# Keys, values and x rows in longer runs, routing buffers and list weights moved, in an attention and mixture-of-experts kernel

## The chip, the cores and the metric

The program runs on one core of a Trainium2 chip. The metric is the device time of one execution in microseconds (us), the median of the runs shown. The core has TensorE (PE, with PEld for its weight loads), VectorE (DVE), ScalarE (ACT), GpSimd (POOL) and SyncE (SP). Each engine works through its own queue in order. Plain transfers are issued by SyncE here, indirect ones by GpSimd; all of them share 16 transfer engines.

## The reference

Attention with 32 memory slots for each of 8 batches and 8 heads (576 positions, 64 values a head), and then a layer of 8 experts in which each of the 4608 rows goes to its two best. Softmaxes and the noise of the gate are cut short here.

```python
a   = softmax(phi, over the positions)               # 8 x 8 x 576 x 32
k_m = einsum('bhsm,bhsd->bhmd', a, k)                # 32 x 64 a head
v_m = einsum('bhsm,bhsd->bhmd', a, v)
x   = softmax(q @ k_m.T / 8) @ v_m                   # rows of 8 * 64 = 512
noisy = x @ w_gate + log1p(exp(x @ w_noise)) * noise # 4608 x 8
top2  = the two largest of noisy, weights by softmax
for e in range(8):
    h = maximum(x[rows of e] @ w1[e], 0)             # 512 -> 1024
    out[rows of e] += weight * (h @ w2[e])           # 1024 -> 512
```

## The kernel before

**Attention.** The work runs over 16 units `u` (a batch and half of its heads). `a_load` brings keys and values of a unit into `kvs` (1 MB and a rest of 128 KB), `p_load` phi, `q_load` q. `a_exp`, `a_tr1`, `a_tr5`, `a_kv` make the slots' keys `kk` and values `vm`; `a_kt` and `a_g` transpose them and multiply the values by the gate's matrix (`a_g`: one product of 128x64, a mask `gt`, a sum over heads); `a_s` makes the scores. Two batches form a pair P (four pairs). Over 20 groups `n` of rows (five a pair) `c_sc`, `c_soft1`, `c_soft2`, `c_tr` do the softmax, and `c_av` makes a block `j` of 128 rows of x (`xr`), with the gate's 16 logits beside it, writes the rows to `xs` in DRAM and adds the logits of both halves into `lg`. A pair has 9 blocks, so there are 36 x writes.

**Routing.** `gate(P, j0, j1)` finds the two best experts of each row of a pair and the row's place in the expert's list (`gidx`), and puts row number and weight into `gent`. Then GpSimd scatters them into the list `lst` in DRAM, two indirect transfers a block: 18 for a pair, and for the last pair 10 and 8 in two calls. `gidx` and `gent` lie in the pool `gs`, which has one buffer.

**Experts.** `lists` reads an expert's list back (`lt`), `gather` fetches its rows from `xs` (`gtile`, GT tiles), halves them into two f16 parts (`ghalf`) and transposes them by a transfer into `xt`. `mm1` is the first layer (L678), `mm2` the second (L705), `put` adds the result to `out` by an indirect transfer (L728). `wt` scales the list's weights (`wlu`). `w_load` and `w_prep` bring an expert's weights (`stg`) and split them into two f16 parts `wh`, `wl` (L569, L570), after a maximum (`wam`, L555) and its scale (`wsa` to `wsc`). The groups 0, 1 and 2 of expert 0 (two tiles each, which need the lists of the first pairs only) are computed while the attention and the routing still run; group 3 (the rest of expert 0) needs the whole list, and all further groups follow it.

**What sets the order.** `unit`, `group`, `weights`, `routing` and `early` give every step a due time from the table `PRI`; the steps are written in that order and a scheduler places the instructions in each engine's queue by priority. `BUF` sets the numbers of buffers and, in `zg`, `zr`, `r0`, `r1`, `m0` to `m2`, after which attention group zero writes, weight splits and early groups may start (`after`). `zero_out` writes zeros to the whole output, 256 KiB each; the first TRASH rows of `xs` and `out` take entries that no row fills.

## Time and profile before

| | us |
|---|---|
| median of 3 runs (lowest, highest) | 1042.14 (1041.88, 1044.54) |
| the profiled execution | 1048.34 |
| its span, first to last instruction | 1046.5 |
| TensorE busy | 962.7 (92%) |
| VectorE busy | 535.2 (51%) |
| ScalarE busy | 370.5 (35%) |
| GpSimd busy | 298.4 (29%) |

Shares of a whole span hide the stages: the attention fills about the first 195 us, the early groups of expert 0 run between 196 and 285 us, and the rest is the experts. Where the profile names a wait, it names the time an engine stood idle in front of an instruction and what ended that. Source lines are those of the kernel before; in the new one they are up to 12 higher.

### The profile page before, as it was taken

The page shows a single profiled execution, that of the slowest core. Times are in us where ns is not written, and L with a number is a line of the kernel's source. Part 1 is how long each engine was busy: PE and PEld are TensorE (multiplying, and loading weights), DVE is VectorE, ACT ScalarE, POOL GpSimd, SP SyncE. Part 2 cuts the span into 40 slices and gives each one's busy share as a digit, 9 for nine tenths or more (in the row PEclk, how much of TensorE's full clock was granted, in tenths as well). Part 3 has the DMA queues.
Part 4 walks back from the last instruction along what each step waited for, and adds up shares of the span by engine and source line. Part 5 has one row for each costly group of instructions (what it writes and reads, how often), then busy time and mean ns, then how long its engine had stood idle before and what let it go on. Part 6 is the DMA issues. An engine that isn't in the chain of part 4 may idle for free.

```text
span 1046.5 us, 15053 instructions
## 1 busy us (share of the span) xinstructions
PE 962.7 (92%) x5632; PEld 500.4 (48%) x5632; DVE 535.2 (51%) x1395; ACT 370.5 (35%) x760; POOL 298.4 (29%) x262
## 2 busy tenths in 40 slices
PE   4898975895799998999999999999999999999995
PEld 3555643563344445444644464445444544454452
DVE  2578888535476254984272349544523682232211
ACT  3466655313242232532242244324222542221211
POOL 1000633776246304222323132223132213211121
PEclk9699977798899999999999999999999999999998
DMA  9999999555988439756546257845453626430221
GB/s 291 331 327 327 267 330 302 113 118 84 238 148 196 95 37 176 204 129 100 107 131 110 42 91 206 170 88 82 131 101 78 124 57 110 66 51 11 31 32 25
DMA packets 143642, 147.93 MB, mean 141 GB/s; under 512 B 92944, under 2 KB 102224, under 8 KB 143568
## 3 DMA queue, kind: packets, MB, share of 16 engines
q1 hardware_dynamic: 124112, 107.02, 39.9%
q0 software_dynamic: 19456, 39.93, 22.0%
q8 instruction: 45, 0.74, 0.3%
q14 instruction: 29, 0.24, 0.1%
HBM read 86.77 MB, written 40.22 MB: 121 GB/s over the span
## 4 chain that ended last, share of the span: by engine, by line
PE 56%; DMA 8%; issue 6%; DVE 6%; POOL 2%; ACT 1%; SPq 0%; POOLq 0%; ACTq 0%; DVEq 0%
PE mp L678 27%; PE ps L705 27%; DMA xt<-ghalf 3%; DVE wl L570 2%; DMA lst<-gent,gidx 2%; DVE wam L555 2%; PE ps L715 2%; DMA stg<-in_w 2%; DMA out<-y,lt 1%; POOL out L728 1%; POOL lst L514 1%; DVE ghalf L654 1%; DVE hl L686 0%; ACT ghalf L651 0%; DVE hh L685 0%
## 5 line engine op out<-in xcount | busy, mean ns | idle before, releaser
L678 PE MATMUL mp<-xt,wh 128*128 128x512 f16 (+2 forms) x1408 | 280.2, 336 | 11.3 <-issue 6.6
L678 PEld LDWEIGHTS <-wh 128*128 128x128 f16 x1600 | 152.5, 99 | 143.6 <-issue 26.6
L728 POOL DMA_INDIRECT out<-y,lt x80 | 128.7, 1609 | 259.8 <-ACT y L709 231.9
L705 PE MATMUL ps<-wh,hl 128*128 128x512 f16 x528 | 200.0, 379 | 1.6 <-DVE hl L686 1.6
L705 PE MATMUL ps<-wl,hh 128*128 128x512 f16 x528 | 199.8, 379 | 0.0
L685 DVE CAST hh<-r 128x512 f16<-128x512 f32 (+3 forms) x200 | 72.1, 364 | 248.8 <-ACT r L684 247.7
L705 PE MATMUL ps<-wh,hh 128*128 128x512 f16 x528 | 195.5, 379 | 1.3 <-DVE hh L685 1.3
L640 POOL DMA_INDIRECT gtile<-xs,lt x80 | 91.0, 1138 | 332.5 <-DVE ghalf L654 292.0
L684 ACT ACTIVATE r<-mp 128x512 f32<-128x512 f32 (+3 forms) x200 | 97.0, 492 | 246.9 <-PE mp L678 175.4
L705 PEld LDWEIGHTS <-hh 128*128 128x128 f16 x1152 | 112.3, 98 | 135.1 <-DVE hh L685 4.6
L678 PE MATMUL mp<-xt,wl 128*128 128x512 f16 (+2 forms) x704 | 151.4, 337 | 0.0
L654 DVE TENSOR_TENSOR ghalf<-gtile,ghalf 128x512 f16<-128x512 f32 x80 | 55.1, 691 | 126.1 <-ACT ghalf L651 125.9
L686 DVE TENSOR_TENSOR hl<-r,hh 128x512 f16<-128x512 f32 (+3 forms) x200 | 111.3, 562 | 4.6
L651 ACT ACTIVATE ghalf<-gtile 128x512 f16<-128x512 f32 x80 | 50.0, 628 | 170.7 <-DMA xt<-ghalf 155.6
L514 POOL DMA_INDIRECT lst<-gent,gidx x72 | 73.0, 1014 | 129.3 <-DVE pe L385 102.8
L678 PEld LDWEIGHTS <-wl 128*128 128x128 f16 x800 | 76.9, 99 | 58.6 <-issue 1.3
L705 PEld LDWEIGHTS <-hl 128*128 128x128 f16 x576 | 56.3, 98 | 74.7 <-issue 5.7
L555 DVE TENSOR_REDUCE wam<-stg 128x1 f32<-128x512 f32 x128 | 81.1, 678 | 20.4 <-DMA stg<-in_w 20.2
L709 ACT ACTIVATE y<-ps,wlu 128x512 f32<-128x512 f32 x66 | 44.7, 681 | 125.0 <-PE ps L705 92.0
L570 DVE SCALAR_TENSOR_TENSOR wl<-stg,wsc,wh 128x512 f16<-128x512 f32 x112 | 76.4, 743 | 1.9 <-ACT wh L569 1.7
L569 ACT ACTIVATE wh<-stg,wsc 128x512 f16<-128x512 f32 x112 | 70.1, 708 | 14.2 <-DVE wsc L336 13.8
L417 PE MATMUL xp<-vb,at 128*128 128x272 f32 (+1 forms) x160 | 50.6, 477 | 14.7 <-ACT xr L419 14.0
(160 smaller groups left out, 723.2 us busy)
## 6 DMA issues: line engine op xcount, KB each, us to landing
stg<-in_w SPq DMA_DIRECT2D x64, 512.0 KB
kvs<-in_kv SPq DMA_DIRECT2D x16, 1024.0 KB
out<-zt SPq DMA_DIRECT2D x38, 256.0 KB
qs<-in_q_t SPq DMA_DIRECT2D x16, 576.0 KB
xs<-xr SPq DMA_DIRECT2D x36, 256.0 KB
phs<-in_phi_t SPq DMA_DIRECT2D x16, 288.0 KB
kvs<-in_kv SPq DMA_DIRECT2D x16, 128.0 KB
gtile<-xs,lt POOLq DMA_INDIRECT x80
```

What stands on the lines that cost most here:

```text
L514: sc = G.indirect_dma_start(out=lst[:, :], out_offset=bass.IndirectOffsetOnAxis(ap=idx[:, j, k:k + 1], axis=0), in_=ent[:, j, k, :], in_of ...
L555: d = V.tensor_reduce(am[:, c:c + 1], ss[c], axis=AX.X, op=OP.max, apply_absolute_value=True)
L569: A.activation(wh[:, cs], ss[c], AF.Identity, scale=sc)
L570: V.scalar_tensor_tensor(wl[:, cs], ss[c], sc, wh[:, cs], op0=OP.mult, op1=OP.subtract)
L640: G.indirect_dma_start(out=gts[i][:n], out_offset=None, in_=xs[0:seen, :], in_offset=bass.IndirectOffsetOnAxis(ap=LT[e][:n, t, 0:1].bitcas ...
L654: V.tensor_tensor(gh[:n, 1], gts[i][:n], gh[:n, 0], OP.subtract)
L678: d = mark["mm1", g if e == 0 else None] = T.matmul(ps[:, :n], ww[:, c * FF + f * 128:c * FF + (f + 1) * 128], xt[:, xo + c, :n], start=(k ...
L684: A.activation(r[:, :n], ps[:, :n], AF.Relu, scale=HC)
L685: V.tensor_copy(hh[:, f, :n], r[:, :n])
L686: V.tensor_tensor(hl[:, f, :n], r[:, :n], hh[:, f, :n], OP.subtract)
L705: T.matmul(ps, hs[:, i * 128:(i + 1) * 128], ws, start=(k == 0), stop=(k == 8 * m - 1))
L728: d = G.indirect_dma_start(out=out[:, :], out_offset=bass.IndirectOffsetOnAxis(ap=LT[e][:n, t, 0:1].bitcast(I32), axis=0), in_=y[:n], in_o ...
```

## The change

Keys and values are laid out on the host so that one partition's four rows of a unit are one run of 8 KB (they were four runs of 2 KB); x rows are written as one run of 2 KB (they were two of 1 KB), for which the logits of one half stand ahead of the values and those of the other behind them; TRASH is 128 instead of 256. `a_g` makes four products of 32 rows by 16 columns and one copy, in place of the product, mask and sum. The first five normalisations of the softmax (GN) run on GpSimd; GL and GV are 0 and move nothing. `gidx` and `gent` have three buffers, `gtile` four. `wt` for expert 0's last tiles is written behind the first layer of group 3. `PRI` and some pacing numbers of `BUF` (`zg`, `zr`, `m1`, `r0`, `r1`) have other values.

```diff
-TRASH = 256
+TRASH = 128
-BUF = dict(kvs=3, phs=3, qs=2, et=2, es=3, pe=4, at=3, xr=4, st0=1, st1=1, ptr=3, px=2, mps=3, xa=3, w1=8, w2=8, zg=9,
-           ws=1, m0=16, m1=18, m2=19, r0=6, r1=6, zr=5)
+BUF = dict(kvs=3, phs=3, qs=2, et=2, es=3, pe=4, at=3, xr=4, st0=1, st1=1, ptr=3, px=2, mps=3, xa=3, w1=8, w2=8, zg=8,
+           ws=1, m0=16, m1=19, m2=19, r0=14, r1=3, zr=6)
...
-GT = 3
+GT = 4
+GN, GL, GV = 5, 0, 0
...
-        nc.sync.dma_start(kvs[:, 0:4], kv[b, 0:512, g].rearrange("(c p) h x -> p c h x", p=128))
-        nc.sync.dma_start(kvs[:64, 4], kv[b, 512:576, g])
+        nc.sync.dma_start(kvs[:, 0:4].rearrange("p c h x -> p (c h x)"),
+                          kv[b, g, 0:512].rearrange("(p c) x -> p (c x)", c=4))
+        nc.sync.dma_start(kvs[:64, 4].rearrange("p h x -> p (h x)"), kv[b, g, 512:576])
...
-        T.matmul(p4[:, 0, 0:64], VT[u], wg_sb[:, g, :], start=True, stop=True)
-        gt = sm.tile([128, 4, 16], F32, name="gt")
-        V.tensor_tensor(gt, p4[:, 0, 0:64].rearrange("p (h c) -> p h c", h=4), vmask[:, :, 0:16], OP.mult)
         vb = wk.tile([128, 272], F32, name="vb", bufs=8)
-        V.tensor_reduce(vb[:, 256:], gt.rearrange("p h c -> p c h"), axis=AX.X, op=OP.add)
+        for h in range(4):
+            T.matmul(p4[h * 32:(h + 1) * 32, 0, 0:16], VT[u][:, h * 32:(h + 1) * 32],
+                     wg_sb[:, g, h * 16:(h + 1) * 16], start=True, stop=True)
+        A.activation(vb[:, 0:16] if g == 0 else vb[:, 256:], p4[:, 0, 0:16], AF.Copy)
...
-        V.tensor_tensor(pe[:, 0:k], pe[:, 0:k], ss[:, 0:k, None].to_broadcast([128, k, M]), OP.mult)
+        (G if n < GN else V).tensor_tensor(pe[:, 0:k], pe[:, 0:k], ss[:, 0:k, None].to_broadcast([128, k, M]), OP.mult)
...
-        nc.sync.dma_start(xs[r0:r0 + 128, :].rearrange("p (g d) -> p g d", g=2), xr[:, :, 0:256])
+        nc.sync.dma_start(xs[r0:r0 + 128, :], xr[:, 16:528])
...
-        idx = gs.tile([128, NJ, 2], I32, name="gidx")
-        ent = gs.tile([128, NJ, 2, 2], F32, name="gent")
+        idx = gs.tile([128, NJ, 2], I32, name="gidx", bufs=3)
+        ent = gs.tile([128, NJ, 2, 2], F32, name="gent", bufs=3)
...
-        if e == 0 and t1 <= 6:
+        if e == 0:
             after(d, "mm1", t0 // 2)
...
     lists(0, 6, NTL + 1)
-    wt(0, 6, NTL + 1)
...
         for f in range(8):
             mm1(e, g, f)
             step_side(2)
+        if (e, g) == (0, 3):
+            wt(0, 6, NTL + 1)
```

The table of due times moves instructions in every queue. Three places show what the prediction speaks of.

SyncE's queue at the first list read of expert 0 (`lt<-lst 128x2x2`), before: `xs<-xr` are x writes, `out<-zt` zero writes, the transposes those of group 0.

```order
L150 DMA out<-zt 128x512 x5
L423 DMA xs<-xr 256x1x256 x2
L150 DMA out<-zt 128x512
L423 DMA xs<-xr 256x1x256
L150 DMA out<-zt 128x512 x2
L593 DMA lt<-lst 128x2x2 x2
L423 DMA xs<-xr 256x1x256 x2
L655 DMA_TRANSPOSE stg<-ghalf 128x8x128 x2
```

The same place after:

```order
L153 DMA out<-zt 128x512 x5
L431 DMA xs<-xr 128x512
L153 DMA out<-zt 128x512
L431 DMA xs<-xr 128x512
L601 DMA lt<-lst 128x2x2 x2
L431 DMA xs<-xr 128x512 x4
L663 DMA_TRANSPOSE stg<-ghalf 128x8x128 x2
```

Counted from the queue's start, the list read stands behind 31 x writes and 38 zero writes before, and behind 27 and 37 after; ahead of group 0's transposes stand two x writes more than before.

GpSimd's queue from the gathers of group 0 to the last scatters, before: `gent` is the counter that starts a routing's entries, `lst<-gent,gidx` the scatters, `out<-y,lt` the adds to the output.

```order
L640 DMA gtile<-xs,lt 128x512 x3
L514 DMA lst<-gent,gidx 37888x2 x13
L640 DMA gtile<-xs,lt 128x512
L514 DMA lst<-gent,gidx 37888x2 x5
L495 IOTA gent 128x10
L514 DMA lst<-gent,gidx 37888x2 x10
L728 DMA out<-y,lt 4864x512
L640 DMA gtile<-xs,lt 128x512 x2
L728 DMA out<-y,lt 4864x512
L495 IOTA gent 128x8
L514 DMA lst<-gent,gidx 37888x2 x8
```

And after:

```order
L522 DMA lst<-gent,gidx 37888x2 x18
L503 IOTA gent 128x8
L648 DMA gtile<-xs,lt 128x512 x4
L522 DMA lst<-gent,gidx 37888x2 x28
L648 DMA gtile<-xs,lt 128x512 x2
L736 DMA out<-y,lt 4736x512 x2
L522 DMA lst<-gent,gidx 37888x2 x8
L648 DMA gtile<-xs,lt 128x512 x3
L648 DMA gtile<-xs,lt 64x512
```

The counters have moved ahead of the gathers, and the scatters of the third pair and of the first part of the last pair stand in one row.

VectorE's queue around the scaling of expert 0's last list weights (`wlu<-lt,wu 128x3` and `64x1`), before:

```order
L555 TENSOR_REDUCE wam<-stg 128x1 x4
L654 TENSOR_TENSOR ghalf<-gtile,ghalf 128x512
L561 TENSOR_REDUCE wam_3802<-wam 128x1
L617 TENSOR_SCALAR wlu<-lt,wu 128x3
L331 TENSOR_REDUCE wsa<-pb 128x1
L332 TENSOR_SCALAR wsa<-wsa 128x1
L621 TENSOR_SCALAR wlu<-lt,wu 64x1
L334 TENSOR_SCALAR wsb<-wsa 128x1
L336 TENSOR_SCALAR wsc<-wsb 128x1
L570 SCALAR_TENSOR_TENSOR wl_3814<-stg,wsc,wh_3813 128x512 x3
```

And after (the part of 128x3 stands further back, behind six of group 3's eight casts):

```order
L339 TENSOR_SCALAR wsc<-wsb 128x1
L693 CAST hh<-r 128x256
L694 TENSOR_TENSOR hl<-r,hh 128x256
L578 SCALAR_TENSOR_TENSOR wl_3829<-stg,wsc,wh_3828 128x512 x2
L625 TENSOR_SCALAR wlu<-lt,wu 128x2
L578 SCALAR_TENSOR_TENSOR wl_3829<-stg,wsc,wh_3828 128x512 x6
L693 CAST hh<-r 128x256 x2
L694 TENSOR_TENSOR hl<-r,hh 128x256 x2
L629 TENSOR_SCALAR wlu<-lt,wu 64x1
L662 TENSOR_TENSOR ghalf<-gtile,ghalf 128x512
```

The scale and the split of expert 1's first weights now stand ahead of the first scaling that needs the last list.

## Rows read from the trace of the kernel before

**Rows 1.** Windows: engines' busy us (and instructions), granted clock, transfer share, GB/s.

```profile
core 0: us, PE busy (x) PEld busy (x) DVE busy (x) ACT busy (x) POOL busy (x), PEclk, DMA share, GB/s
125.00:165.00 40.00, 32.00 (x236) 19.30 (x234) 35.18 (x135) 22.74 (x59) 21.06 (x23) 0.83 1.09 308
165.00:180.00 15.00, 7.05 (x21) 3.54 (x21) 14.04 (x49) 9.02 (x21) 3.52 (x4) 0.75 1.05 332
275.00:300.00 25.00, 18.35 (x87) 8.71 (x86) 14.77 (x28) 5.71 (x10) 7.42 (x7) 0.86 1.08 238
325.00:350.00 25.00, 25.00 (x128) 11.28 (x127) 13.47 (x25) 7.37 (x13) 9.84 (x7) 1.00 0.53 91
500.00:600.00 100.00, 100.00 (x532) 49.14 (x531) 41.36 (x82) 29.47 (x52) 26.18 (x21) 1.00 0.48 96
```

**Rows 2.** Timeline of SyncE: start, duration, transfer issued.

```profile
179.30 1.09 SPq L593 DMA_DIRECT2D lt<-lst  x2
180.50 9.12 SPq L423 DMA_DIRECT2D xs<-xr  x2
```

**Rows 3.** Timeline of GpSimd, with the idle time ahead and what ended it.

```profile
184.83 1.00 POOL L640 DMA_INDIRECT gtile<-xs,lt  x1 [9.79 <-DMA lt<-lst]
...
188.66 1.00 POOL L514 DMA_INDIRECT lst<-gent,gidx  x1 [0.30 <-issue]
189.97 0.98 POOL L514 DMA_INDIRECT lst<-gent,gidx  x1 [0.30 <-issue]
...
211.98 0.96 POOL L514 DMA_INDIRECT lst<-gent,gidx  x1 [0.31 <-issue]
214.73 0.14 POOL L495 IOTA gent<- 128x10 int32 x1 [1.79 <-DMA lst<-gent,gidx]
215.69 0.98 POOL L514 DMA_INDIRECT lst<-gent,gidx  x1 [0.82 <-DVE gai L501]
...
235.15 1.00 POOL L514 DMA_INDIRECT lst<-gent,gidx  x1 [0.28 <-POOL gent L495]
...
244.87 0.97 POOL L514 DMA_INDIRECT lst<-gent,gidx  x1 [0.31 <-issue]
...
253.28 1.01 POOL L640 DMA_INDIRECT gtile<-xs,lt  x1 [5.51 <-DMA lt<-lst]
```

**Rows 4.** Timeline of VectorE: indices of two routings, and the list's scaling.

```profile
182.46 0.18 DVE L502 CAST gidx<-gai 128x18 int32<-128x18 f32 x1
...
232.68 0.17 DVE L502 CAST gidx<-gai 128x8 int32<-128x8 f32 x1 [6.83 <-DMA lst<-gent,gidx]
...
252.36 0.23 DVE L617 TENSOR_SCALAR wlu<-lt,wu 128x3 f32<-128x3 f32 x1 [9.85 <-DMA lt<-lst]
```

**Rows 5.** Timeline of TensorE and ScalarE: first matmul, a result, waits.

```profile
196.05 1.04 PE L678 MATMUL mp<-stg,wh 128*128 128x256 f16 x4 [1.30 <-DMA stg<-ghalf]
...
219.39 0.69 ACT L709 ACTIVATE y<-mp,wlu 128x512 f32<-128x512 f32 x1 [3.58 <-PE mp L705]
...
253.39 1.95 ACT L569 ACTIVATE wh<-stg,wsc 128x512 f16<-128x512 f32 x3 [9.94 <-DVE wsc L336]
...
255.65 1.01 PE L678 MATMUL mp<-stg,wh 128*128 128x256 f16 x4 [5.61 <-ACT r L684]
...
285.60 1.65 PE L678 MATMUL mp<-xt,wh 128*128 128x448 f16 x4 [6.65 <-issue]
```

**Rows 6.** Groups by line and form: busy us, mean ns, idle before.

```profile
L275 PE MATMUL tr<-kvs,es 128*32 128x128 f32 x512 | 22.4, 322 | 8.9 <-DMA kvs<-in_kv 6.7 <-DVE gt L320 1.4 <-DVE kb L296 0.9
L396 DVE TENSOR_TENSOR pe<-pe,ss 128x512 f32<-128x512 f32 x16 | 11.0, 686 | 0.1
L294 ACT ACTIVATE vt<-tr 64x128 f32<-64x128 f32 x16 | 4.2, 265 | 0.3 <-PE tr L292 0.2
L322 DVE TENSOR_REDUCE vb<-gt 128x16 f32<-128x64 f32 x16 | 4.0, 252 | 0.0
L320 DVE TENSOR_TENSOR gt<-tr,vmask 128x64 f32<-128x64 f32 x16 | 3.5, 221 | 4.1 <-PE tr L318 4.0
```

**Rows 7.** Transfer queue in 10:55, 140:145, 165:180 us: packets, MB, share.

```profile
q1 hardware_dynamic: 6921, 14.83, 104.2%
...
q1 hardware_dynamic: 968, 2.05, 104.5%
...
q1 hardware_dynamic: 3440, 4.93, 103.1%
```

More of the change, by code (lines that the diff above doesn't have):

```diff
@@ L27 @@
 TAIL = CAP - NTL * 128
[L28 removed]
+TRASH = 128
 ZC = 512
 ZERO_AT = 20
[L31 to L38 removed]
+PRI = dict(D=5.82512, p=-1.14871, kv=-1.26659, q=-2.4532, exp=-1.09005, tr1=-2.82213, tr5=-2.85978, kvm=0.83783,
+           kt=1.0766, s=2.13563, g=2.0709, v=3.89957, v1=2.83229, sc=-2.28787, s1=-0.02984, s2=0.281, tr=-0.49952,
+           av=1.31436, avb=1.42743, gate=0.6, g2=0.5622, gs=0.99413, x0=0.22977, md=0.72156, md1=0.2297, fill=5.7433,
+           prep=2.87573, prd=0.4427, wl=1.01221, wl3=3.40386, pr1=6.05278, z=4.13465, zd=0.20212, d0=-1.38568,
+           d1=-0.31647, d2=0.35338, d3=-0.20179, sc0=1.77362, sc1=-0.24397, sc2=-0.03774, sc3=0.13919, f0=0.11614,
+           f1=0.2, g0=1.24719, g1=0.39992, prep0=3.62472, prd0=0.55109)
+BUF = dict(kvs=3, phs=3, qs=2, et=2, es=3, pe=4, at=3, xr=4, st0=1, st1=1, ptr=3, px=2, mps=3, xa=3, w1=8, w2=8, zg=8,
+           ws=1, m0=16, m1=19, m2=19, r0=14, r1=3, zr=6)
 NEED = (1, 1, 2)
[L41 removed]
+GT = 4
 HC = 2.0 ** -14
 WEXP = 2.0 ** 9
+GN, GL, GV = 5, 0, 0
 SBITS = float((2 * 127 + 9) << 23)
@@ L355, in a_v @@
         for g in range(2):
-            vb = VB[2 * b + g][:, 0:256].rearrange("p (h d) -> p h d", h=4)
+            vb = VB[2 * b + g][:, 16 - 16 * g:272 - 16 * g].rearrange("p (h d) -> p h d", h=4)
             vm = VM[2 * b + g]
-            V.scalar_tensor_tensor(vb, vm[:, None, :].to_broadcast([128, 4, D]), s, vmask, op0=OP.mult, op1=OP.mult)
+            if b < GV:
+                G.tensor_scalar(vm, vm, s, None, op0=OP.mult)
+                G.tensor_tensor(vb, vm[:, None, :].to_broadcast([128, 4, D]), vmask, OP.mult)
+            else:
+                V.scalar_tensor_tensor(vb, vm[:, None, :].to_broadcast([128, 4, D]), s, vmask, op0=OP.mult, op1=OP.mult)
     JS = ((0, 1), (2, 3), (4,), (5, 6), (7, 8))
@@ L412, in c_av @@
             LG[P] = wk.tile([128, NJ, 16], F32, name="lg")
-        xr = wk.tile([128, 2, 272], F32, name="xr", bufs=BUF["xr"])
+        xr = wk.tile([128, 544], F32, name="xr", bufs=BUF["xr"])
         for g in range(2):
@@ L916, in layout @@
     a["phi_t"] = c(phi.reshape(B, 2, 4, S, M).transpose(0, 2, 4, 1, 3).reshape(B, 128, 2, S))
-    a["kv"] = c(np.concatenate([k[..., None, :], v[..., None, :]], axis=-2)
-                .reshape(B, 2, 4, S, 2 * D).transpose(0, 3, 1, 2, 4))
+    x = (np.concatenate([k[..., None, :], v[..., None, :]], axis=-2)
+         .reshape(B, 2, 4, S, 2 * D).transpose(0, 1, 3, 2, 4).reshape(B, 2, S, 8 * D))
+    y = x[:, :, :512].reshape(B, 2, 4, 128, 8 * D).transpose(0, 1, 3, 2, 4).reshape(B, 2, 512, 8 * D)
+    a["kv"] = c(np.concatenate([y, x[:, :, 512:]], axis=2))
     a["wgn"] = c(np.concatenate([moe_w_gate, moe_w_noise], axis=1)
```

12 lines of the change are left out of this document (3 added, 9 removed).

## The prediction

> **What bounds the kernel now.** I read the windows first. From 325 us TensorE is busy for all of every stretch but a few gaps (25.00 of 25 and 100.00 of 100 in two such windows) [rows 1], and its matmuls are the same in both kernels. That block can only begin earlier, so the question is how early the work ahead of it is done. In 275 to 300 us TensorE has only 18.35 of 25 us: it has run out of the early groups of expert 0 and waits for group 3, whose first matmul is at 285.60 after 6.65 us of idle time [rows 5].
>
> So I followed group 3 backwards. It needs the complete list of expert 0, hence the last scatter. GpSimd issues that one at 244.87 and the first gather at 253.28 [rows 3]. Before that GpSimd's own queue is what ends last: from the first gather at 184.83 to the first scatter of the last routing at 235.15 it has 28 scatters, 4 gathers, 2 gathers and 2 adds to the output, nearly all in steps of 1.28 us (0.97 us and 0.30 us between two). It starts at 184.83 because the list read issued at 179.30 [rows 2] has landed only then: GpSimd had waited 9.79 us [rows 3].
>
> What holds the list read? SyncE issues in order, and 31 x writes and 38 zero writes stand ahead of it. The transfer engines are full throughout: a share of 1.09 in 125 to 165 us and 1.05 in 165 to 180 us, at 308 and 332 GB/s [rows 1]. VectorE is the other candidate: 35.18 of 40 us and 14.04 of 15 [rows 1], with the indices of the third routing out at 182.46 [rows 4], just in time for the scatter at 188.66 [rows 3].
>
> **The change, part by part.** The sum is made against the profiled execution, 1048.34 us (span 1046.5), which lies 6.2 us over the median of 1042.14; I take the same difference off at the end.
>
> *The list read comes earlier.* In the new order 27 x writes and 37 zero writes stand ahead of it. That is 4 x writes and one zero write of 256 KiB less, and the rows of zeros for the trash are 256 KiB instead of 512: 6 × 0.262 MB = 1.57 MB, at 308 GB/s 5.1 us. The two edits to run lengths come on top. The trace has a price for a byte at different run lengths: the packets' share times the stretch times 16 engines, over the bytes. With loads of about 2.1 KB a packet (10 to 55 us) this is 1.042 × 45 × 16 / 14.83 = 50.6 engine-us a MB; with writes of about 1.4 KB (165 to 180 us) 1.031 × 15 × 16 / 4.93 = 50.2 [rows 7]. The length of a run shows no price there. The best stretch, 140 to 145 us, in which weights come in runs of 4 KB, has 1.045 × 5 × 16 / 2.05 = 40.8 [rows 7]. So keys and values (16.8 MB) save between nothing and 16.8 × 9.8 / 16 = 10.3 us, and 27 x writes (7.08 MB, from 50.2) between nothing and 4.2 us. A loss has no mechanism but a small transfer that stands behind one long packet, 8 KB at 50 ns a KB, 0.4 us. I take 3 us in all, near the low end, since two of the three rows say nothing. Term: −8 us, from −4 to −20.
>
> The Trainium skill, "DMA: Bandwidth & Descriptors", section Specifications, gives 512 B as the least transfer for line rate. By that rule both kernels are at line rate and longer runs give nothing, which would make this term −5 and the whole −10; the two equal prices of [rows 7] are on its side, the third row against it.
>
> Does GpSimd have the indices by then? It would reach the first scatter of the third routing at about 182 instead of 188.66. Its indices were out at 182.46. VectorE has less to do before them: 16 products and 16 reductions of the gate go (0.221 and 0.252 us each, 7.6 us), and five of the normalisations move to GpSimd (four of 0.686 and one of half the size, 3.1 us) [rows 6]. GpSimd is idle at that time, and nothing but the first scatters stands behind them. Of those 10.7 us I count half as earlier indices, 177, so they don't hold the scatters. What replaces the gate products: 16 ScalarE copies of 128x16, of which the nearest row is 0.265 us for 64x128, 4.2 us on an engine with 22.74 of 40 us; and 64 products of 32 rows by 16 columns, each in two passes, at 22.4 / 512 = 44 ns (the products with 32 rows) [rows 6] 5.6 us on TensorE, about what the old ones took. Both are spread over 180 us and lie beside the transfers; if that cover failed they would cost their 4 to 6 us.
>
> *Three routing buffers.* Today the index and entry tiles exist once, so each routing waits for the transfers of the one before. GpSimd issues a scatter at 211.98 and the next only at 215.69: 2.4 us more than a normal step. VectorE stands 6.83 us until the last indices at 232.68 [rows 3, 4]; GpSimd covers that with two gathers and two adds. In the new order the 28 scatters stand in one row with 2 gathers and 2 adds behind them, the entry counters are filled earlier, and the same 36 scatters, 6 gathers and 2 adds are left. Term: −2.6 us, from 0 to −4. The fourth gather tile (GT = 4) lets the four gathers of group 3 go out together; it is in the next term.
>
> *Late list weights.* After the last scatter VectorE waits 9.85 us at 252.36 for the list, to scale it. Behind that wait stand the scale of expert 1's weights, then ScalarE's cast of them (it waited 9.94 us), then ScalarE's evacuations of group 2's first layer, and TensorE stands still for 5.61 us [rows 4, 5]. The new order has these weight casts ahead, but one scaling of the list's tail (64x1) still stands ahead of group 2's casts and group 3's halves, so VectorE still waits there; only the weights are out of the way. The scaling that moved waits for the last matmul of group 3's first layer; behind it stand casts for the second layer, which TensorE can begin without. Most of TensorE's 5.61 us isn't on the path, since TensorE has 6.65 us idle later for group 3. What is on the path is ScalarE's and VectorE's first halves of group 3, about 2 us behind the weights. Term: −2 us, from 0 to −6.
>
> Sum: −8 − 2.6 − 2 = −12.6, say −13: 1035 in a profiled execution, and 1042.1 − 13 = **1029 us** as the median. TensorE doesn't take the bound back: it would start the early groups some 8 us earlier too (196.05 in [rows 5]), and loses its gap of 5.61 us, so it is still ahead of group 3.
>
> **The rivals.** *The attention stage itself moves.* If the long runs get the price of the best stretch, the first term is −20; GpSimd's 50 us then begin near 165 and the sum is −20 − 2.6 − 2, some −24, less what VectorE then fails to follow (its indices at 177 allow a first scatter 11.7 us earlier, not 20): −16 to −22, about 1023. For it: shares over 1.0. Against: the equal prices of [rows 7].
>
> *The list read isn't what holds.* If the indices of the third routing don't come earlier than 182.46, or zeros and x writes still end near 179 since VectorE paces both, only 4 to 6 us are left of the three terms: 1037. For it: VectorE's 14.04 of 15 us.
>
> *Nothing.* The three terms are each taken back by the next queue: 1042, within 0.3% (3.1 us), which is about what a measurement of this kernel can tell from no change.
>
> *Slower: the first transposes come late.* Group 0's transposes stand in SyncE's queue behind four x writes of the last pair instead of two, and today two x writes take 9.12 us there [rows 2]. If four take 18 us or more, TensorE, in order, stands before group 0's first layer, and six products of the last attention blocks stand behind it. The two adds to the output stand in GpSimd's queue ahead of the last 8 scatters and need group 0's results. Today the second result starts at 219.39, 23 us after the first matmul at 196.05 [rows 5]; GpSimd would come to the adds at 177 + 5 + 36 + 3 = 221. A first matmul 2 us later than today makes GpSimd wait, and one 16 us later than today eats all that the sum gives; at 20 us later the time is 1046. For it: the row of 9.12 us. Against: the list read ahead of them goes out earlier, and these x writes come from attention blocks that don't wait for it.
>
> **How the numbers follow.** Forecast, 1024 to 1034: 0.47 (the rule on run length, 1032, lies inside). Attention moves, 1015 to 1024: 0.17. The list read isn't it, 1034 to 1039: 0.18. Nothing: 0.10. Slower: 0.08. The range from 1018 to 1040 leaves out about a fifth: the far part of the second case, half of *nothing* and the slower one. Faster by over 0.3%: 0.82; within: 0.10; slower: 0.08.
>
> **What would show it.** In the new profile the list read goes out near 171 and GpSimd's first gather near 177; scatters run in steps of 1.28 us without the gap at 215; the last one is out near 234; group 3's first matmul is near 272; TensorE is full from about 312. VectorE's share falls by some 11 us before 180, and the transfers' price of the loads stays near 50 engine-us a MB if run length has no price. I'm wrong if the first gather still waits until 183, if the two adds wait for TensorE ahead of the last scatters, or if a new gap in TensorE stands after 325.

## The result and the profile after

| | kernel before | changed kernel |
|---|---|---|
| median, us (lowest, highest), 14 runs each | 1042.46 (1037.58, 1047.35) | 1036.92 (1032.22, 1040.55) |
| ratio, 95% interval | | 0.9934 (0.9916 to 0.9953) |
| profiled execution, us (span) | 1048.34 (1046.5) | 1032.22 (1030.4) |

The change makes the kernel about 0.7% faster, 5.5 us by the medians and 6.9 by the ratio, where I forecast 13. Single runs of either kernel spread over some 9 us, and the two profiled executions are at opposite ends of their spreads: the traces differ by 16 us, of which 9 to 11 are no work of the change. So I use the traces for the order of events and the ratios for times. 1% is 10.4 us. Runs more than 1.5% over the fastest of the same kernel count in no ratio, and the trace of the changed kernel's first repeat, which is such a run, is read for its early rows alone.

The windows of the changed kernel (columns as in [rows 1]):

```profile
core 0: us, PE busy (x) PEld busy (x) DVE busy (x) ACT busy (x) POOL busy (x), PEclk, DMA share, GB/s
10.00:55.00 45.00, 36.87 (x430) 23.25 (x430) 26.62 (x89) 29.08 (x87) 4.82 (x5) 1.00 1.03 371
125.00:165.00 40.00, 25.53 (x230) 17.20 (x229) 30.59 (x102) 19.25 (x48) 17.59 (x19) 0.81 1.03 281
165.00:180.00 15.00, 7.51 (x24) 4.44 (x25) 14.23 (x54) 9.79 (x22) 2.61 (x3) 0.60 0.82 290
250.00:275.00 25.00, 22.34 (x128) 13.32 (x128) 14.26 (x31) 7.52 (x16) 11.97 (x11) 0.93 1.10 267
275.00:300.00 25.00, 21.57 (x110) 10.50 (x108) 20.43 (x47) 12.49 (x22) 9.94 (x7) 1.00 1.15 158
300.00:325.00 25.00, 22.82 (x111) 10.45 (x110) 13.26 (x24) 6.66 (x11) 10.79 (x9) 0.93 0.83 186
325.00:350.00 25.00, 25.00 (x117) 11.32 (x116) 9.16 (x16) 6.66 (x11) 4.20 (x4) 1.00 0.36 71
```

The stretch from 275 to 300 us has 21.57 us of TensorE's work instead of 18.35, but the next one still has a hole. TensorE is full from about 314 us (its last wait ends at 313.48), not from 312 as forecast but near it. Between 165 and 180 us the transfers are no longer full (0.82 instead of 1.05), while VectorE has 14.23 of 15 us.

SyncE, GpSimd and VectorE, the rows that answer to [rows 2 to 4]:

```profile
171.73 1.10 SPq L601 DMA_DIRECT2D lt<-lst  x2
173.38 5.69 SPq L431 DMA_DIRECT2D xs<-xr  x4
```

```profile
176.78 1.01 POOL L648 DMA_INDIRECT gtile<-xs,lt  x1 [14.80 <-DMA xs<-xr]
...
180.60 0.95 POOL L648 DMA_INDIRECT gtile<-xs,lt  x1 [0.30 <-issue]
185.77 0.99 POOL L522 DMA_INDIRECT lst<-gent,gidx  x1 [4.22 <-DVE gidx L510]
...
237.71 1.03 POOL L522 DMA_INDIRECT lst<-gent,gidx  x1 [0.30 <-issue]
246.69 0.98 POOL L648 DMA_INDIRECT gtile<-xs,lt  x1 [7.96 <-DMA lt<-lst]
```

```profile
181.59 0.69 DVE L662 TENSOR_TENSOR ghalf<-gtile,ghalf 128x512 f16<-128x512 f32 x1 [0.84 <-ACT ghalf L659]
...
184.31 0.69 DVE L662 TENSOR_TENSOR ghalf<-gtile,ghalf 128x512 f16<-128x512 f32 x1 [1.69 <-ACT ghalf L659]
184.92 0.22 DVE L509 TENSOR_REDUCE gai<-gu 128x9 f32<-128x72 f32 x1
185.06 0.22 DVE L509 TENSOR_REDUCE gai<-gln 128x9 f32<-128x72 f32 x1
185.31 0.18 DVE L510 CAST gidx<-gai 128x18 int32<-128x18 f32 x1
```

The list read goes out 7.6 us earlier and the first gather 8.0 us earlier, as forecast (171 and 177). How much of this is the change's, one trace of the kernel before can't say: a kernel with the same order up to there has its list read at 177.90 in one trace and at 171.14 in another (three buffers alone, below). The first scatter of the third routing is only 2.9 us earlier. GpSimd is there at about 181.9 and waits 4.22 us for the indices, and VectorE has them late because two second halves of group 0 stand ahead of them in its queue and wait, behind ScalarE's first halves, for the gathers. The 28 scatters then run without the gap that [rows 3] shows at 214.73; the last one is 7.2 us earlier than in [rows 3].

TensorE's first product of group 0, and its longer waits after that (answering to [rows 5]):

```profile
188.59 1.06 PE L686 MATMUL mp<-stg,wh 128*128 128x256 f16 x4
...
227.30 0.47 PE L332 MATMUL pb<-identf,wam 128*128 128x128 f32 x1 [6.89 <-DVE wam L569]
...
251.18 0.60 PE L686 MATMUL mp<-stg,wh 128*128 128x256 f16 x4 [3.01 <-ACT r L692]
269.02 0.92 PE L686 MATMUL mp<-xt,wh 128*128 128x448 f16 x4 [1.48 <-ACT ghalf L659]
281.14 0.92 PE L686 MATMUL mp<-xt,wh 128*128 128x448 f16 x4 [2.78 <-ACT r L692]
...
313.48 0.64 PE L723 MATMUL ps<-wh,hh 128*64 128x512 f16 x2 [2.18 <-ACT y L717]
```

Group 3's first product is at 269.02 instead of 285.60 and waits 1.48 us instead of 6.65. In its place stands a wait that was not there: 6.89 us at 227.30, for the maxima of expert 1's weights, whose reductions now stand early in VectorE's queue and wait there for the load.

### The profile page after: what moved, and what is told of

It is laid out like the page before. It is cut to its first block, busy times and chain, and to the rows that moved or that the text cites. A ratio compares the mean times of both kernels' runs of the same rounds, so it can differ in the third digit from the quotient of the medians.

```text
span 1030.4 us, 15239 instructions
## 1 busy us (share of the span) xinstructions
PE 947.8 (92%) x5728; PEld 496.2 (48%) x5728; DVE 529.9 (51%) x1358; ACT 373.0 (36%) x776; POOL 291.8 (28%) x267
## 4 chain that ended last, share of the span: by engine, by line
PE 60%; DMA 6%; issue 5%; DVE 3%; POOL 1%; ACT 1%; SPq 0%; POOLq 0%; ACTq 0%
PE mp L686 30%; PE ps L713 28%; DMA xt<-ghalf 4%; PE ps L723 2%; DMA out<-y,lt 1%; DVE wl L578 1%; POOL out L736 1%; DVE ghalf L662 1%; DVE wam L563 0%; DMA stg<-in_w 0%; DMA gtile<-xs,lt 0%; ACT ghalf L659 0%; DMA lst<-gent,gidx 0%; DMA lt<-lst 0%; DVE hh L693 0%
## 5 line engine op out<-in xcount | busy, mean ns | idle before, releaser
L713 PE MATMUL ps<-wh,hh 128*128 128x512 f16 x528 | 195.3, 379 | 0.0
L648 POOL DMA_INDIRECT gtile<-xs,lt x80 | 82.3, 1029 | 316.3 <-DVE ghalf L662 277.2
L662 DVE TENSOR_TENSOR ghalf<-gtile,ghalf 128x512 f16<-128x512 f32 x80 | 54.8, 689 | 114.0 <-ACT ghalf L659 113.9
L522 POOL DMA_INDIRECT lst<-gent,gidx x72 | 70.9, 984 | 69.3 <-DVE gidx L510 30.9
L425 PE MATMUL xp<-vb,at 128*128 128x272 f32 (+1 forms) x160 | 49.3, 465 | 16.1 <-ACT xr L427 14.0
```

The source lines that it names most:

```text
L522: sc = G.indirect_dma_start(out=lst[:, :], out_offset=bass.IndirectOffsetOnAxis(ap=idx[:, j, k:k + 1], axis=0), in_=ent[:, j, k, :], in_of ...
L648: G.indirect_dma_start(out=gts[i][:n], out_offset=None, in_=xs[0:seen, :], in_offset=bass.IndirectOffsetOnAxis(ap=LT[e][:n, t, 0:1].bitcas ...
L662: V.tensor_tensor(gh[:n, 1], gts[i][:n], gh[:n, 0], OP.subtract)
L713: T.matmul(ps, hs[:, i * 128:(i + 1) * 128], ws, start=(k == 0), stop=(k == 8 * m - 1))
```

## The experiments

After the result there were three theories. **Theory one** is the prediction's own: the earlier list read is worth most, the buffers 2.6 us, late weights 2. **Theory two**: the three buffers, with the moves that they allow, are the whole gain. **Theory three**: the buffers are worth more than the whole, and the rest costs. Each experiment has its ratio to the kernel before, measured on the same chip beside it; several edits also make the scheduler rewrite parts of the order, which is said where it happens. "Numbers" are the values in the tables `PRI` and `BUF`.

| kernel | ratio to the kernel before | 95% interval |
|---|---|---|
| changed kernel | 0.9934 | 0.9916 to 0.9953 |
| the same again (two more times) | 0.9907, 0.9926 | 0.9883 to 0.9932, 0.9895 to 0.9956 |
| changed, short runs | 0.9918 | 0.9886 to 0.9950 |
| changed, weights early | 0.9937 | 0.9911 to 0.9964 |
| changed, one routing buffer | 1.0013 | 0.9990 to 1.0037 |
| changed, gate work on VectorE | 1.0044 | 1.0017 to 1.0071 |
| changed, old numbers | 0.9939 | 0.9914 to 0.9965 |
| changed, indices first | 0.9900 | 0.9865 to 0.9935 |
| before, three routing buffers (twice) | 0.9880, 0.9881 | 0.9838 to 0.9922, 0.9842 to 0.9921 |
| before, three buffers and less on VectorE | 0.9912 | 0.9879 to 0.9945 |
| before, new numbers | 1.0156 | 1.0123 to 1.0189 |

**The changed kernel again**, twice, unchanged.

> The changed kernel once more, unchanged, for a second trace and more times. The pair of traces so far differs by 16 us, their medians by 5.5. Theory one (the pair shows an ordinary gain and two unlucky ends of the scatter): time 1037 +- 1.5 as median; in the trace the first gather again at 177 +- 2, the last scatter at 238 +- 2, group 3's first matmul between 268 and 278, the wait of TensorE of 6.9 us at 220 again. Rival (the place of group 3 is chance): the list milestones repeat within 2 us, but group 3's first matmul, or expert 1's first evacuation (320.0 us in the first trace), lies 5 us or more elsewhere.

> The changed kernel a third time, beside the three below on the same chip. All theories: 0.9915 +- 0.003 of the kernel before.

Measured 0.9907 and 0.9926. The gain is there each time; the middle of the three, 0.9926, is 7.7 us. The trace of the first repeat has the list read at 170.61; that of the second has it at 169.30, the last scatter at 235.63, group 3's first evacuation (ScalarE's copy of a first-layer result) at 273.7 and the new wait again (7.54 us at 224.10).

**Short runs.** The longer runs taken back, all engines with the same instructions in the same order:

```
-        nc.sync.dma_start(kvs[:, 0:4].rearrange("p c h x -> p (c h x)"),
-                          kv[b, g, 0:512].rearrange("(p c) x -> p (c x)", c=4))
+        nc.sync.dma_start(kvs[:, 0:4], kv[b, 0:512, g].rearrange("(c p) h x -> p c h x", p=128))
...
-        nc.sync.dma_start(xs[r0:r0 + 128, :], xr[:, 16:528])
+        nc.sync.dma_start(xs[r0:r0 + 128, :].rearrange("p (g d) -> p g d", g=2),
+                          xr.rearrange("p (g d) -> p g d", g=2)[:, :, 16:272])
```

> The changed kernel with the run lengths of the kernel before and nothing else: keys and values loaded in runs of 2 KB (host array laid out as before), x rows read from the tile in two halves of 1 KB each. All engines have the same instructions in the same order. Theory one (run length is worth what the load stage showed, 331 against 371 GB/s in 10 to 55 us): the loads there fall back to about 331 GB/s, the list read goes out 2 to 4 us later (174 to 176 instead of 171.7), the time is 2 to 4 us over the changed kernel, about 1040. Rival one (length has no price, the rate differed for another reason): 0 +- 1, list read near 172. Rival two (the attention stage moves as a whole with the rate): 10 us later list read, time 1044 or more. Rival three (the list read moves but the indices on VectorE hold the scatters): list read 2 to 4 us later, first scatter of the third routing still at 186 +- 1, time 0 +- 1.

Measured 0.9918, beside 0.9907 for the changed kernel in the same comparison: no price within 3 to 4 us. The transfer queue in 10 to 55 us (packets, MB, share), first with short runs, then the changed kernel, and the list read with short runs:

```profile
q1 hardware_dynamic: 7972, 16.19, 104.1%
```

```profile
q1 hardware_dynamic: 4762, 16.61, 102.7%
```

```profile
172.26 1.25 SPq L601 DMA_DIRECT2D lt<-lst  x2
```

By the reckoning of the prediction these are 46.3 and 44.5 engine-us a MB: with 2.0 instead of 3.5 KB a packet on average, a MB costs 4% more. The list read is 0.5 to 3 us later than in the changed kernel's three traces, the first scatter of the third routing (186.23) 0.5 us later than in its first. So in this order lengths have no price in time that shows, by rival one or by rival three, which I can't tell apart. By the Trainium skill, "DMA: Bandwidth & Descriptors", section Specifications, runs of 512 B and more are at line rate; in this order these runs agree with it to within those 4%. The 50.6 of [rows 7], at the same 2 KB, is then not the length's doing alone. I don't know what else it is: with short runs, four traces in the old order had 331 to 340 GB/s in that stretch, the kernel before with the new numbers 331, the changed kernel 361. And in the old order there is a difference by length: of the two kernels there with less on VectorE (below), the one with short runs moved 334 GB/s and the one with long runs 358. They differ in other edits too, and their times show no gain from it (0.9912 and 0.9939).

**Weights early.** The scaling of the last list weights is back at its old place; on the engines this moves one VectorE instruction (and swaps a few weight loads of TensorE).

```
-        if (e, g) == (0, 3):
-            wt(0, 6, NTL + 1)
...
+    wt(0, 6, NTL + 1)
     seq = [(0, 3)] + [(e, g) for e in range(1, E) for g in range(3)]
```

> The changed kernel with the scaling of expert 0's last list weights (128x3) back at its place ahead of group 3. In the order of instructions this moves one VectorE instruction alone: it stands right ahead of the scaling of the list's tail (64x1), ahead of group 3's halves, instead of between group 3's evacuations. Theory one (late weights are worth 2 us): 2 us over the changed kernel. Rival (the tail's scaling waits at that place for the same list, 6.3 us in the changed kernel's trace, so the one beside it adds no wait): 0 +- 1, VectorE's wait for the list 6 to 7 us as before, only now named with the 128x3 one.

Measured 0.9937, beside 0.9907 (intervals that overlap). VectorE with weights early:

```profile
246.44 0.23 DVE L625 TENSOR_SCALAR wlu<-lt,wu 128x3 f32<-128x3 f32 x1 [7.18 <-DMA lt<-lst]
246.61 0.20 DVE L629 TENSOR_SCALAR wlu<-lt,wu 64x1 f32<-64x1 f32 x1
```

The rival's reason shows: the wait is about the same (7.18 us), and the tail's scaling, which did not move, would have it anyway. The times can't tell 0 from 3 us; the trace gives no place for 2.

**One routing buffer** in the changed kernel; the scheduler then writes the last two routings and expert 1's reductions in another order.

```
-        idx = gs.tile([128, NJ, 2], I32, name="gidx", bufs=3)
-        ent = gs.tile([128, NJ, 2, 2], F32, name="gent", bufs=3)
+        idx = gs.tile([128, NJ, 2], I32, name="gidx")
+        ent = gs.tile([128, NJ, 2, 2], F32, name="gent")
```

> The changed kernel with one buffer instead of three for the routing's indices and entries. The scheduler moves a few instructions: the index casts of the last two routings stand later in VectorE's queue, and the reductions of expert 1's weights no longer stand ahead of the last indices. Theory one (the buffers are worth the gap in GpSimd's row of scatters and VectorE's wait): a gap of 2 to 3 us returns between the 18th and the 19th scatter after 185 us, the last scatter is 2 to 3 us later (240 to 241), the time 2 to 3 us over the changed kernel. Rival (GpSimd's row has slack ahead of its last 8 scatters, which wait for the adds): 0 +- 1. Second rival (the reductions that moved matter more: TensorE's 6.9 us at 220 go): 0 to 4 us faster.

Measured 1.0013: 11 us over the changed kernel in the same comparison, and all of its gain gone. GpSimd, VectorE, TensorE and ScalarE:

```profile
210.30 0.14 POOL L503 IOTA gent<- 128x10 int32 x1 [2.84 <-DMA lst<-gent,gidx]
211.27 1.00 POOL L522 DMA_INDIRECT lst<-gent,gidx  x1 [0.82 <-DVE gden L514]
...
241.31 0.97 POOL L522 DMA_INDIRECT lst<-gent,gidx  x1 [0.30 <-issue]
```

```profile
228.98 0.17 DVE L510 CAST gidx<-gai 128x8 int32<-128x8 f32 x1 [11.17 <-DMA lst<-gent,gidx]
```

```profile
232.14 1.01 PE L686 MATMUL mp<-stg,wh 128*128 128x256 f16 x4 [9.89 <-ACT r L692]
```

```profile
231.19 0.63 ACT L659 ACTIVATE ghalf<-gtile 128x512 f16<-128x512 f32 x1 [12.39 <-DMA gtile<-xs,lt]
231.72 0.64 ACT L692 ACTIVATE r<-mp 128x256 f32<-128x256 f32 x2
...
255.11 4.39 ACT L577 ACTIVATE wh<-stg,wsc 128x512 f16<-128x512 f32 x7 [1.00 <-DVE wsc L339]
```

The gap in the scatters (3.5 us) and the last scatter's delay (3.6 us, although the list read, at 169.65, is 2.1 us earlier) are little more than expected. What I had not priced is who stands behind them. The index cast on VectorE waits 11.17 us for the scatters that read the one buffer, and behind it stand casts of group 1's results. TensorE stops for 9.89 us, 3 us longer than in the changed kernel at this place. But VectorE is free again at 229; the wait that ends last, at 231.19, is ScalarE's: 12.39 us for the gathers of group 2, which stand in GpSimd's queue behind the scatters and their gap, with group 1's evacuations behind it. The casts of expert 1's weights, at 232 us in the changed kernel, are back behind the wait for the list, at 255. Which of the two makes up the 11 us was not separated.

**Three buffers alone**, in the kernel before: the same two lines of it with `bufs=3`, nothing else.

> The kernel before with three buffers instead of one for the routing's indices and entries, and nothing else (table, layouts and gate products stay). The scheduler then writes the last indices earlier and moves the reductions and casts of expert 1's weights ahead of the wait for the list, as the whole change does. Theory two (the buffers, with what they let the scheduler move, are the whole gain): 5 to 8 us faster than the kernel before, 1034 to 1037; list read still near 179, first scatter of the third routing still near 188, no gap between the 18th and 19th scatter after it, last scatter 2 to 4 us earlier than 244.87. Theory one (the earlier list read is worth most, the buffers 2.6): 2 to 3 us faster. Rival (nothing without the table): 0 +- 1.

> The kernel before with three routing buffers and nothing else, a second time, now beside the whole change. Theory two (the buffers, with the moves they allow, are the whole gain, and the rest of the change sums to about nothing): within 3 us of the changed kernel, either side, about 0.990 of the kernel before. Theory three (the rest of the change costs): 4 us or more faster than the changed kernel. Theory one (the first measure was chance; buffers are worth 2.6 us): 0.9975.

Measured 0.9880 and 0.9881, some 12.5 us each time; in the second comparison the whole change has 0.9926. VectorE, ScalarE and GpSimd of the first:

```profile
218.13 0.15 DVE L502 CAST gidx<-gai 128x8 int32<-128x8 f32 x1
...
250.80 0.23 DVE L617 TENSOR_SCALAR wlu<-lt,wu 128x3 f32<-128x3 f32 x1 [7.71 <-DMA lt<-lst]
```

```profile
222.77 5.00 ACT L569 ACTIVATE wh<-stg,wsc 128x512 f16<-128x512 f32 x8
```

```profile
239.02 0.97 POOL L514 DMA_INDIRECT lst<-gent,gidx  x1 [0.30 <-issue]
```

Its list read, and that of the second trace of the same kernel:

```profile
177.90 1.09 SPq L593 DMA_DIRECT2D lt<-lst  x2
```

```profile
171.14 1.10 SPq L593 DMA_DIRECT2D lt<-lst  x2
```

The wait of 6.83 us at the last index cast [rows 4] is gone, the cast is 14.6 us earlier, and expert 1's weights are cast at 222.77 instead of 253.39 [rows 5]: ahead of the list's wait, which is still there (7.71 us) and now has little behind it. Theory one falls. Theory two gave the size to within some 4 to 5 us; theory three fits the second comparison, but the two intervals overlap, so that the rest of the change costs 4 to 5 us is likely and not shown. The list read shows what one trace is worth: the same program has it 6.8 us apart, with SyncE's, VectorE's and ScalarE's queues up to there in the order of the kernel before (179.30).

**The new numbers alone**: the kernel before with the changed tables of priorities and buffers.

> The kernel before with the new table of priorities and buffer numbers, and nothing else: one routing buffer, short runs, gate products on VectorE, weights early. Theory one (the order puts the list read ahead of four x writes and a zero write): list read 4 to 6 us earlier than 179.30, first gather at 180 +- 2, time 3 to 5 us faster. Theory two (buffers are the whole gain): list read earlier too, but time 0 +- 2, since the row of scatters has its gap again and the last scatter stands near 242. Rival (the table was found for the other kernel and is worse here): 3 us slower or more.

Measured 1.0156, 16 us slower, with the list read at 187.60, 8 us *later* than before. The numbers by themselves are bad, as the rival said. VectorE and TensorE:

```profile
202.84 0.18 DVE L502 CAST gidx<-gai 128x18 int32<-128x18 f32 x1
...
248.72 0.17 DVE L502 CAST gidx<-gai 128x8 int32<-128x8 f32 x1 [12.77 <-DMA gtile<-xs,lt]
```

```profile
252.17 1.01 PE L678 MATMUL mp<-stg,wh 128*128 128x256 f16 x4 [10.94 <-ACT r L684]
```

**Gate work on VectorE** in the changed kernel: one gate product a unit, masked and summed on VectorE, and no normalisation on GpSimd. The order changes from the attention on.

```
-GN, GL, GV = 5, 0, 0
+GN, GL, GV = 0, 0, 0
...
-        for h in range(4):
-            T.matmul(p4[h * 32:(h + 1) * 32, 0, 0:16], VT[u][:, h * 32:(h + 1) * 32],
-                     wg_sb[:, g, h * 16:(h + 1) * 16], start=True, stop=True)
-        A.activation(vb[:, 0:16] if g == 0 else vb[:, 256:], p4[:, 0, 0:16], AF.Copy)
+        T.matmul(p4[:, 0, 0:64], VT[u], wg_sb[:, g, :], start=True, stop=True)
+        gt = sm.tile([128, 4, 16], F32, name="gt")
+        V.tensor_tensor(gt, p4[:, 0, 0:64].rearrange("p (h c) -> p h c", h=4), vmask[:, :, 0:16], OP.mult)
+        V.tensor_reduce(vb[:, 0:16] if g == 0 else vb[:, 256:], gt.rearrange("p h c -> p c h"), axis=AX.X, op=OP.add)
```

> The changed kernel with the gate products as before (one product of 64 columns a unit, masked and summed on VectorE) and all normalisations on VectorE. Some 10.7 us more of VectorE's work before 180 us. Theory one (VectorE's load sets when the indices of the third routing come, half of it counts): first scatter of the third routing 3 to 5 us later than 185.77, time 3 to 5 us over the changed kernel. Rival one (the transfers pace the attention stage, VectorE has slack): list read and first scatter within 1.5 us of the changed kernel, time 0 +- 1.5. Rival two (the normalisations on GpSimd cost more than they free): first list read earlier, time 1 to 3 us faster.

Measured 1.0044, some 12 us over the changed kernel, three times what theory one gave. GpSimd and VectorE:

```profile
196.35 1.00 POOL L522 DMA_INDIRECT lst<-gent,gidx  x1 [7.59 <-DVE gidx L510]
...
249.39 1.03 POOL L522 DMA_INDIRECT lst<-gent,gidx  x1 [0.30 <-issue]
```

```profile
195.39 0.18 DVE L510 CAST gidx<-gai 128x18 int32<-128x18 f32 x1
```

In the new order VectorE's load does hold the attention stage: the indices of the third routing come 10 us later and everything after them with them. The list read is later too, at 178.56, so this run doesn't tell the indices from the stage as a whole.

**The old numbers in the changed kernel**, and **three buffers and less on VectorE in the kernel before** (short runs, old numbers). The first sets the two tables back; the second puts the small gate products, ScalarE's copies of them and `(G if n < 5 else V)` at the normalisation into the kernel with three buffers.

> The changed kernel with the priorities and buffer numbers of the kernel before: long runs, three routing buffers, less work on VectorE, late weights, fewer trash rows, in the old order. Theory (new numbers and less work on VectorE belong together: the new numbers alone cost the kernel before 16 us, VectorE's old work costs the new order 12): without the new numbers the list read is at 176 +- 3, the time 0 to 5 us over the changed kernel. Rival one (the numbers are worth nothing, VectorE's relief gives its gain in any order): within 2 us of the changed kernel, list read before 174. Rival two (the old numbers are better with relief): 3 us faster or more.

> The kernel before with three routing buffers, the small gate products (four of 32 rows by 16 columns a unit, evacuated by ScalarE) and five normalisations on GpSimd; short runs, old numbers, old trash rows, weights early. Theory (VectorE paces the attention stage in any order): list read 3 to 6 us earlier than 177.9, last scatter at 234 to 236, time 3 to 5 us under the one with buffers alone. Rival (in the old order the transfers pace it: the list read waits for zeros and x writes): list read 177 +- 1.5, time within 2 us of the one with buffers alone. Rival two (ScalarE, which took the copies, is late with the x rows): slower by 2 us or more.

Measured 0.9939 and 0.9912, beside 0.9926 for the changed kernel and 0.9881 for three buffers alone. With VectorE relieved, the new numbers are worth nothing that shows (rival one), although they cost 16 us without the relief; and in the old order the relief shows no gain. The two belong together and about cancel each other. The old numbers gave the earliest list of all, the last scatter at 229.34, 15.5 us ahead of the kernel before, and no more time than the rest. Its TensorE then waited elsewhere, in the middle of group 3's first layer: behind ScalarE, which waited for the transposes of group 3 before it could write the next half, with a result and the evacuations behind that. ScalarE, then TensorE:

```profile
284.98 0.63 ACT L659 ACTIVATE ghalf<-gtile 128x512 f16<-128x512 f32 x1 [13.84 <-DMA xt<-ghalf]
285.51 0.67 ACT L717 ACTIVATE y<-mp,wlu 128x512 f32<-128x512 f32 x1
```

```profile
286.23 1.65 PE L686 MATMUL mp<-xt,wh 128*128 128x448 f16 x4 [6.75 <-ACT y L717]
```

**Indices first.** In the changed kernel the halves of group 0 wait for the indices of the third routing, and expert 1's first reductions for group 1's first layer; the scheduler moves two weight loads behind the list reads as well.

```
-            V.tensor_tensor(gh[:n, 1], gts[i][:n], gh[:n, 0], OP.subtract)
+            after(V.tensor_tensor(gh[:n, 1], gts[i][:n], gh[:n, 0], OP.subtract), "idx", 2 if (e, g) == (0, 0) else None)
...
-            if e == 0 and c == 0:
-                after(d, "av", BUF["r%d" % i])
+            if (e == 0 and c == 0) or (e, i) == (1, 0):
+                after(d, *(("mm1", 1) if e else ("av", BUF["r%d" % i])))
...
-        V.tensor_copy(idx[:, 0:nj].rearrange("p j k -> p k j"), ai)
+        mark["idx", P] = V.tensor_copy(idx[:, 0:nj].rearrange("p j k -> p k j"), ai)
```

> The changed kernel with two more dependences, both on VectorE: the second halves of group 0 wait for the index cast of the third routing (in the changed kernel two of them stand ahead of it and wait for the gathers), and the reductions of expert 1's first weights wait for the last product of group 1's first layer (in the changed kernel four of them stand ahead of the last indices and wait for the load). Theory (the indices of the third routing, late behind the halves, hold GpSimd's row: 185.31 where 182 was possible): first scatter of the third routing at 182 +- 1 instead of 185.77, the last one at 234 +- 1.5 instead of 238, TensorE's wait of 5 to 7 us at 220 gone, time 3 to 6 us under the changed kernel, 1030 to 1033. Rival one (TensorE's work for groups 0 to 2 is then done earlier and it only waits longer for group 3, which hangs on its transposes and the weight loads beside them): scatters earlier as said, time 0 +- 1.5. Rival two (group 0 late, since its halves wait): first matmul of group 0 after 192, the adds to the output hold GpSimd ahead of the last scatters, time 2 us slower.

Measured 0.9900: 0.7 to 3.5 us under the changed kernel's three measurements, at least two of them on other chips, with intervals that overlap. That decides nothing between the theory's 3 to 6 us and rival one. GpSimd, ScalarE and TensorE:

```profile
183.29 1.35 POOL L522 DMA_INDIRECT lst<-gent,gidx  x1 [0.30 <-DVE gidx L510]
...
233.39 0.96 POOL L522 DMA_INDIRECT lst<-gent,gidx  x1 [0.30 <-issue]
```

```profile
226.97 0.63 ACT L659 ACTIVATE ghalf<-gtile 128x512 f16<-128x512 f32 x1 [10.55 <-DMA gtile<-xs,lt]
227.50 0.37 ACT L692 ACTIVATE r<-mp 128x256 f32<-128x256 f32 x1
```

```profile
227.92 1.01 PE L686 MATMUL mp<-stg,wh 128*128 128x256 f16 x4 [8.06 <-ACT r L692]
```

GpSimd's wait of 4.22 us for the indices is gone and the scatters are earlier as said, but TensorE stands still at the same place and longer. The wait for the weights' maxima is gone, and behind it comes the next: ScalarE waits 10.55 us for the gathers of group 2, which stand in GpSimd's queue behind the 28 scatters, and group 1's evacuations stand behind that on ScalarE.

## Why the prediction was half right

The sign and the range held; the size was half, and the sum had the wrong terms. That the total came out inside the range is in part luck: the term of −8 us brought nothing that shows, and the one of −2.6 more than the whole. The path of each trace can be cut into four pieces that add up to its span: up to group 0's first product, TensorE's idle time from there to the first evacuation of expert 1, its work in that stretch, and the rest. Worked out from the timelines:

| kernel | group 0's first product | idle to expert 1 | work to expert 1 | the rest | last scatter at |
|---|---|---|---|---|---|
| before | 196.1 | 21.6 | 114.7 | 714.1 | 244.9 |
| changed | 188.6 | 17.4 | 114.0 | 710.4 | 237.7 |
| changed, second trace used | 185.6 | 20.2 | 115.9 | 709.8 | 235.6 |
| changed, one buffer | 186.6 | 29.6 | 121.0 | 708.6 | 241.3 |
| changed, gate work on VectorE | 195.5 | 22.1 | 119.3 | 713.9 | 249.4 |
| changed, old numbers | 186.1 | 21.9 | 118.7 | 707.5 | 229.3 |
| before, three buffers (twice) | 195.3, 188.0 | 16.9, 16.1 | 115.9, 117.2 | 707.8, 708.2 | 239.0, 231.8 |

The rest is about the same work in every kernel (TensorE is busy for 694 to 700 us of it), and I take its 707 to 714 us for the spread of executions: four traces with nearly the same order, the changed kernel twice, with short runs and with weights early, have 709.2 to 713.2. So the table places only some 5 of the buffers' 12.5 us, in TensorE's idle time (21.6 against 16.9 and 16.1). In the second trace group 0 also begins 8.1 us earlier, but in the first only 0.8; where the remainder comes from is not shown.

The column of work differs between the kernels in part because of TensorE's clock, which I left out of the prediction. In the kernel before, group 3's first four products come after 6.65 us of idle time and take 1.65 us [rows 5]; in the changed kernel they come after 1.48 us and take 0.92. The granted clock is 0.66 from 280 to 290 us in the one and 1.00 from 260 to 280 us in the other, where 1.00 is the higher of the two levels (2.4 GHz) and 0.50 the lower (1.2 GHz). Worked out from the granted clock in steps of 1 us, an estimate, the lower level costs 7 us of the 114.7 before, 6 of the 114.0 in the changed kernel, and 6 to 11 in the others of the table. In these rows a wait cost more than its length.

**"The list read comes earlier", −8 us.** The milestones came as forecast: list read 171.73, first gather 176.78, and group 0 begins 7.5 us earlier. But 3 of the 8 us were for run length, which is worth nothing within 3 to 4 us (short runs), and 6.8 us lie between two traces of one program. All kernels in the new order with VectorE relieved have the list read at 169.3 to 173.2, the old order with VectorE's old work at 171.1 to 179.3. Nor does the time follow it: the old numbers with the earliest read of all, 167.96, have 0.9939, three buffers and less on VectorE with 177.21 have 0.9912, both measured beside the same runs of the kernel before. So the time that the earlier read was to bring did not stay.

**"So they don't hold the scatters"** is the first step that failed. I counted half of VectorE's relief as earlier indices, at 177, and they came at 185.31 (182.65 in the second trace used); VectorE's busy time before 180 us fell by 5.1 us (129.1 to 124.0), not by some 11. What stands in the way: group 0's halves, which the earlier gathers set off, are ahead of the indices in VectorE's queue. The relief is worth far more than the nothing that I gave it, 12 us, but only in the new order, where it pays for what the new numbers cost.

**"TensorE doesn't take the bound back"** is the second, and the dearer one. I took the last scatter to set the time of group 3, and group 3 that of the rest. In the kernel before that is so: 244.87, and 6.65 us of waiting at group 3. In the changed kernel group 3's first product waits 1.48 us and the idle time has gone to the evacuations of groups 1 and 2. With the last scatter anywhere from 229.3 to 239.0 us the ratios are 0.988 to 0.994 in no order; with 241, 245, 249 and 259 they are 1.001, 1.000, 1.004 and 1.016. Below some 240 us earlier lists bought nothing in these kernels; the scatter is one trace's each time, and the ratio is of all runs.

**Three buffers, −2.6 us, from 0 to −4**, is the term that was mis-sized: 12.5 us in the kernel before, 11 in the changed one. The gap in the scatters (2.4 us) was rightly read, and VectorE's 6.83 us at the index cast I called covered by GpSimd's gathers and adds. I asked who waits for GpSimd, not who stands behind the waiting cast on VectorE: casts of group 1's results, and the scale and casts of expert 1's weights. In the trace of the kernel before the first of these cost TensorE little (it is idle for 1.8 us from 220 to 240 us), the second 5.61 us at 255.65. **Late list weights, −2 us**: the row that I read, ScalarE's 9.94 us behind the list's wait, was a true cost, and it went because the buffers let expert 1's casts stand ahead of it. The edit that I gave it to did nothing that the trace shows.

Of the rivals, the second (*the list read isn't what holds*, 1037) gives the measured time, and its condition came true: the indices were no earlier than 182.46. But of its three reduced terms one was the whole. The slower rival did not happen: the four x writes ahead of group 0's transposes took 5.69 us, less than the two of [rows 2], and group 0's first product came earlier. *Nothing* is excluded by three measurements.

What stays open: why three buffers alone are no slower than everything together is shown only as a sum, since the parts change each other's order. That the buffers make the gain is shown from both sides; by which waits is in part argued. Whether the scale and casts of expert 1's weights or the evacuations of group 1 carry more of the 12 us was not separated by a run. The casts begin at 214 to 233 us in six kernels that gain, at 253 to 273 in the three with one buffer and at 248 with the gate work on VectorE; but with indices first they begin at 249, and that kernel gains too.

The kernel before with three routing buffers, two edited lines, has the lowest ratio that was measured: 0.9881 beside 0.9926, with intervals that overlap.

## What to carry to other kernels

When a tile exists once, list every instruction that stands behind the write that must wait for it, on that engine, and follow each one to TensorE, and look whether another engine's wait ends later; here the gap that shows at the reader (2.4 us) was the small part. A chain that ends last is worth following only down to the next one: find out from the trace where TensorE will stand when the first wait is gone, and stop counting there. Undo the parts one at a time, and also put them in one at a time: here the numbers alone cost 16 us, the relief gives 12 in their order and nothing that shows in the old one, and the buffers give 11 to 12.5 in both. And take two traces of one program before a milestone is credited to an edit.

## What the runs showed of the hardware

Keys and values in runs of 2 KB moved at 361 GB/s (with the other loads of the stage) where runs of 8 KB moved at 363 to 374 in six traces, all with the same order there; I had read a best stretch at 4 KB as a price of run length, and in this order it was not one. And I had not expected what fills the transfer engines where group 3's transposes run. In the changed kernel, from 250 to 300 us:

```profile
DMA packets 15076, 10.61 MB, mean 212 GB/s; under 512 B 12915, under 2 KB 12915, under 8 KB 15072
```

The windows above have a share of 1.10 and 1.15 for its two halves, at 267 and 158 GB/s. Six packets in seven are under 512 B; by elimination these are the lists and the transposes, beside the next expert's weights. ScalarE's 13.84 us in the kernel with the old numbers ended with such a transpose. Whether moving the weight loads away from it would help was not tried.
